# Strassen's scheme for the last matrix product of an attention and feed-forward kernel

## The chip, the cores and the metric

The kernel runs on one core of a Trainium2 chip. The metric is the device time in microseconds (us) from the start to the end of one execution. The core has a matrix engine (TensorE, PE in the rows; PEld is its weight load), a vector engine (VectorE, DVE), an activation engine (ScalarE, ACT), a general engine (GpSimd, POOL) and a queue that issues the memory transfers (SyncE, SP). Each engine works through its own instructions in a fixed order and waits at semaphores for the others.

## The reference

Attention in chunks of 64 tokens, then two feed-forward blocks on 4608 tokens of width 512:

```python
attn = softmax(q_c @ k_c.T / 8)                      # per head and chunk of 64 tokens
x = (attn @ v_c) as 4608 x 512
x = relu(x @ w_in)**2 @ w_out                        # 512 -> 2048 -> 512
x = (sigmoid(x @ w_gate) * (x @ w_val)) @ moe2_w_out # 512 -> 1536 -> 512
```

All weights come as 64-bit floats (two 32-bit words each), the result is float32. To keep float32 accuracy every operand of a product is split in two parts of a narrower float type, a high part (ScalarE, line 426) and the rest (VectorE, line 431, a subtraction with two inputs in the core's memory), and each product is three matmuls: high by high, low by high, high by low.

## The kernel before

Four products follow each other on TensorE.

- **The first** (`x @ w_in`, line 578, together with attention) runs in units of 384 tokens by Strassen's scheme in Winograd's form: seven block products, named P1 to P7, in place of eight. **The second** (line 932) is a plain product: for each of nine blocks `j` of 512 tokens, over 16 row blocks `f` of the weight, with four sums in four PSUM banks. **The third** (gate and value, line 578 again, units of 512 tokens, and one of 256) is by Strassen's scheme.
- **The last** (line 1041) is plain: for each of nine blocks `j` of 512 tokens, in falling order and block 0 at the end, for each of 12 row blocks `f` of `moe2_w_out`, a 256 KB load of `ud[f, j]` (what the third product wrote), one split, and 12 matmuls: three for each of four groups of 128 tokens. The tokens lie on the output's partitions there, so that the four sums are copied out by ScalarE and VectorE in turn (lines 411 and 1053) and stored as rows of 2 KB.

Weights pass through `to_float32` (lines 473 to 497: a 512 KB load, two operations of ScalarE, three of VectorE, one of GpSimd) and `weight_group`, which makes the Strassen sums of a pair of weight blocks on GpSimd and splits them. Those of the third product's second half and of the last product go back to memory (`through_dram`) and are loaded again when they are needed. Before, three buffers `raws2` take the loaded words in turn, and the float32 result and the sums take what the planner finds free.

What sets the order: the code states jobs (engine, cost, buffers), and `Plan` gives each a due time, counted back from TensorE's jobs, and then plays the engines through in time with estimated costs, to fix the order on each engine and the place of each buffer. A load is not placed before its `look` time ahead of its due time; `FLOOR` is memory kept free of early work. No engine reorders anything at run time.

## Time and profile before

| | us |
|---|---|
| median of 3 runs (1755.51 to 1756.17) | 1755.55 |
| the profiled execution | 1755.8 |
| its span, first to last instruction | 1754.0 |
| TensorE busy in it | 1694.7 |
| VectorE busy | 986.5 |
| ScalarE busy | 810.0 |
| GpSimd busy | 452.4 |
| the 16 transfer engines, mean | 49.7% |

The span is cut into the stretches of the four products: first 0 to 454, a passage to 545, second to 923, third to 1455, last to 1749.5. In a table of stretches each engine's busy time stands with its number of instructions, then the granted clock of TensorE (1.00 is 2.4 GHz), the transfer engines' share and what they moved.

### The profile page before, as it was taken

To read this page: it belongs to the slowest core of one execution; us is meant where nothing else is said; L and a number is where in the kernel's file an instruction comes from. 1 tells how busy PE (TensorE), PEld (TensorE's weight loads), DVE (VectorE), ACT (ScalarE), POOL (GpSimd) and SP (SyncE) were. 2 spreads that over 40 slices of the span, in tenths; PEclk is the share of its full clock that TensorE was granted. 3 is DMA by queue.
4 is the path that set the end of the run, shared out by engine and by line. 5 is a ranking of instruction groups with operands and counts; after the bars stand their busy time and mean duration, and the time that the engine had idled before them with its cause. 6 is when DMAs were issued, how large, how long until landed. Compare 5 with 4: busy or idle time off the path is not lost.

```text
span 1754.0 us, 27689 instructions
## 1 busy us (share of the span) xinstructions
PE 1694.7 (97%) x10200; PEld 1459.2 (83%) x10200; DVE 986.5 (56%) x1494; ACT 810.0 (46%) x1558; POOL 452.4 (26%) x356
## 2 busy tenths in 40 slices
PE   6789999999998999999999999999999999999998
PEld 5689999999996888888889887788788898888887
DVE  7998575766799633222277468563754553223221
ACT  6676565565685422222246445453544442222221
POOL 2653012020335300000047456452553330000000
PEclk8799999999999999999999999999999999999999
DMA  9825645554683544444455453286325553434431
GB/s 252 198 83 158 160 125 144 141 138 141 222 298 123 175 144 120 120 121 120 120 156 194 167 173 133 90 265 232 125 87 192 186 193 124 146 114 133 132 115 60
DMA packets 278488, 268.38 MB, mean 153 GB/s; under 512 B 154448, under 2 KB 204624, under 8 KB 278352
## 3 DMA queue, kind: packets, MB, share of 16 engines
q1 hardware_dynamic: 278352, 266.61, 49.7%
q8 instruction: 80, 1.31, 0.3%
q14 instruction: 56, 0.46, 0.1%
HBM read 164.30 MB, written 102.24 MB: 152 GB/s over the span
## 4 chain that ended last, share of the span: by engine, by line
PE 85%; DVE 6%; issue 2%; ACT 1%; POOL 0%; DMA 0%; DVEq 0%; ACTq 0%; POOLq 0%
PE bank L578 43%; PE bank L932 21%; PE bank L1041 17%; PE bank L722 1%; PE bank L772 1%; PE bank L756 1%; PE bank L705 0%; DVE T__823 L431 0%; DMA ud<-b__9948 0%; DVE T__11440 L431 0%; DVE T__10156 L431 0%; DVE T__10571 L431 0%; POOL yr__11118 L440 0%; DVE T__12200 L431 0%; DMA gd<-b__2780 0%
## 5 line engine op out<-in xcount | busy, mean ns | idle before, releaser
L440 POOL TENSOR_TENSOR raw__487<-raw__630,raw__487 128x384 f32<-128x384 f32 x24 | 27.6, 1170 | 251.8 <-DVE B__641 L431 195.4
L497 POOL TENSOR_TENSOR w__8576<-w__8576,raw__5243 128x512 int32<-128x512 int32 x3 | 4.4, 1454 | 271.4 <-DMA g__6439<-gd 269.7
L740 DVE TENSOR_REDUCE mx__330<-bank 128x8 f32<-128x512 f32 x16 | 11.0, 689 | 20.0 <-PE bank L722 18.3
L1041 PE MATMUL bank<-wo__6252,uop__12855 128*128 128x512 f32 x84 | 20.2, 389 | 0.0
L1041 PEld LDWEIGHTS bank<-wo__6252,uop__12855 128*128 128x128 f32 x84 | 15.8, 188 | 3.3
L497 POOL TENSOR_TENSOR w__5359<-w__5359,raw__5243 128x512 int32<-128x512 int32 x1 | 1.3, 1310 | 58.4 <-DMA gd<-e__4889 58.4
L440 POOL TENSOR_TENSOR raw__630<-raw__630 128x384 f32<-128x384 f32 x12 | 15.4, 1299 | 0.0
L1041 PE MATMUL bank<-wo__12334,uop__13151 128*128 128x512 f32 x60 | 14.4, 389 | 0.0
L1041 PE MATMUL bank<-wo__6128,uop__13397 128*128 128x512 f32 x60 | 14.4, 389 | 0.0
L440 POOL TENSOR_TENSOR raw__487<-raw__487 128x384 f32<-128x384 f32 x12 | 14.1, 1198 | 0.0
L1041 PEld LDWEIGHTS bank<-wo__12334,uop__13151 128*128 128x128 f32 x60 | 11.3, 188 | 2.3
L1041 PEld LDWEIGHTS bank<-wo__6128,uop__13397 128*128 128x128 f32 x60 | 11.3, 188 | 2.3
L787 ACT ACTIVATE raw__630<-bank 128x256 f32<-128x256 f32 x36 | 11.8, 381 | 1.5 <-PE bank L772 1.4
L787 ACT ACTIVATE raw__487<-bank 128x256 f32<-128x256 f32 x36 | 11.9, 383 | 1.0 <-PE bank L772 1.0
L1041 PE MATMUL bank<-wo__6281,uop__13350 128*128 128x512 f32 x48 | 11.5, 389 | 0.0
L1041 PE MATMUL bank<-wo__12297,uop__13135 128*128 128x512 f32 x48 | 11.5, 389 | 0.0
L1053 DVE COPY o__14742<-bank 128x512 f32<-128x512 f32 x1 | 0.7, 691 | 19.0 <-PE bank L1041 19.0
L440 DVE TENSOR_TENSOR b__9797<-b__9797,bank 128x512 f32<-128x512 f32 x6 | 4.1, 684 | 12.2 <-PE bank L578 12.2
L1041 PEld LDWEIGHTS bank<-wo__6281,uop__13350 128*128 128x128 f32 x48 | 9.0, 188 | 1.9
L1041 PEld LDWEIGHTS bank<-wo__12297,uop__13135 128*128 128x128 f32 x48 | 9.0, 188 | 1.9
L932 PE MATMUL bank<-gop__6265,wo__6128 128*128 128x512 f32 x12 | 5.4, 612 | 4.6 <-DVE gop__6265 L431 2.4
L411 ACT ACTIVATE o__13430<-bank 128x512 f32<-128x512 f32 x1 | 0.6, 598 | 19.1 <-PE bank L1041 19.1
(4427 smaller groups left out, 5605.4 us busy)
## 6 DMA issues: line engine op xcount, KB each, us to landing
g__6439<-gd SPq DMA_DIRECT2D x15, 256.0 KB, 2.7
g__6531<-gd SPq DMA_DIRECT2D x15, 256.0 KB, 2.8
g__6507<-gd SPq DMA_DIRECT2D x14, 256.0 KB, 2.9
u__12690<-ud SPq DMA_DIRECT2D x13, 256.0 KB, 3.4
u__12858<-ud SPq DMA_DIRECT2D x13, 256.0 KB, 2.7
g__6618<-gd SPq DMA_DIRECT2D x12, 256.0 KB, 2.6
ql__1102<-in_q_dram SPq DMA_DIRECT2D x80, 36.0 KB, 2.1
g__6732<-gd SPq DMA_DIRECT2D x10, 256.0 KB, 2.7
```

Of the source, the lines that this page charges most:

```text
L411: lambda: nc.scalar.activation(out=o(), in_=i(), func=func, **kw), ib, ob, soon=soon,
L440: eng, cost(eng, n), lambda: e.tensor_tensor(out=o(), in0=a(), in1=b(), op=op),
L497: nc.gpsimd.tensor_tensor(out=wi, in0=wi, in1=words()[:, :, 0], op=ALU.add)
L578: nc.tensor.matmul(out=o, lhsT=at(op, P, F32R, wi * size + half * HB + kk * P), rhs=at(xb, n, F32R, xi * xsize + off), start=(first and kk ...
L722: nc.tensor.matmul(out=o[part, 2 * hp + c, :], lhsT=qv[part, hp, tok], rhs=kv[part, hp, tok], start=True, stop=True,)
L740: job("DVE", 0.7, lambda: nc.vector.tensor_reduce(out=col8(mx, 0), in_=heads(ps), axis=AX.X, op=ALU.max), [ps], [mx])
L756: nc.tensor.transpose(out=at(ps_t, P, F32, hp * P), in_=at(a, P, F32, hp * P), identity=ident)
L772: nc.tensor.matmul(out=o[c][CH * r:CH * r + CH, hp, :], lhsT=vv[part, 2 * hp + r, :], rhs=av[part, hp, r, :], start=True, stop=True,)
L787: nc.scalar.activation(out=o[:, :, a:a + CH], in_=i, func=ACTF.Copy)
L932: nc.tensor.matmul(out=at(ps[m], BLK), lhsT=at(w1out[f], P, F32R, wi * BLK + m * P), rhs=at(op, BLK, F32R, xi * BLK), start=(f == 0 and i ...
L1041: nc.tensor.matmul(out=at(ps[m], BLK), lhsT=at(op, P, F32R, ui * BLK + m * P), rhs=at(wo[f], BLK, F32R, wi * BLK), start=(f == 0 and i == ...
L1053: job("DVE", 0.7, lambda o=o, b=ps[m]: nc.vector.tensor_copy(out=at(o), in_=at(b, BLK)), [ps[m]], [o])
```

## The change

- The last product becomes a Strassen product (`Long`). A unit is a pair of token blocks (512 tokens each) or, for block 0, two halves of 256. Its two weight halves are the row blocks 0 to 5 and 6 to 11 of `moe2_w_out` and its columns 0 to 255 and 256 to 511; each of the seven products runs over six row blocks and adds into two PSUM banks (two groups of 128 output columns), 36 matmuls. The order on TensorE is P1, P4 of the unit before, P2, P5, P6, P3, P7.
- The sums of tokens that the scheme wants are made by GpSimd (`minus`, 24 operations for a unit), and every product splits its own six operands (`x`), 42 splits for a unit.
- The output has its columns on the partitions, so VectorE turns it in blocks of 32 by 32 (line 1177), eight operations for a unit, and each turned tile is stored with four transfers whose pieces are 32 columns (128 bytes) long: 160 transfers and 73,728 pieces in all.
- `moe2_w_out` passes through `weight_group` (split sums, 6 groups of 7 x 256 KB), not `weight_rows`.
- Conversions of the third and last products' weights go through fixed buffers: two for the loaded words, two for the float32 result, one for the sums.
- Planner: the estimated transfer rate rises (190 to 270 GB/s in play, 150 to 200 for due times), `FLOOR` falls from 20 to 8 KB, loads and splits of the second product are placed later (16 and 8 us ahead, not 25), and a load of a token tile counts 25% more bytes.

```diff
-            extra = self.DMA_LATENCY + self.MARGIN + j.bytes / 150e3 if j.eng == "SP" else 0.4
+            extra = self.DMA_LATENCY + self.MARGIN + j.bytes / 200e3 if j.eng == "SP" else 0.4
...
-                dma = max(dma, t) + j.bytes / 190e3
+                dma = max(dma, t) + j.bytes / 270e3
...
-    LOOK, NEAR, HOLD, FAR, FLOOR = 60.0, 15.0, 8.0, 40.0, 20 * 1024
+    LOOK, NEAR, HOLD, FAR, FLOOR = 60.0, 15.0, 8.0, 40.0, 8 * 1024
...
-        raw = sbuf(2 * BLK, "wraw")
+        raw, w = sbuf(2 * BLK, "wraw"), sbuf(BLK, "w")
         if raws:
             turn.append(1)
-            raw = raws[len(turn) % len(raws)]
-        w = sbuf(BLK, "w")
+            raw, w = (x[len(turn) % len(x)] for x in raws[:2])
...
-        sums = sbuf(2 * BLK, "sums")
+        sums = raws[2][0] if raws else sbuf(2 * BLK, "sums")
...
+    class Long:
...
+        def product(self, ps, p, first):
...
+            if p == "P5":
+                self.minus(b11, b12, b11)
+            elif p == "P6":
+                self.minus(b11, b22, b11)
+            elif p == "P7":
+                self.minus(b12, b22, b12)
+            elif p == "P4":
+                self.minus(b21, b21, b11)
+            kind, half = A_OF[p]
+            for kp, r in enumerate(src):
+                x = Buf(8 * n, name="x", op=True)
+                split(x, r, n, look=8.0)
+                w = self.ops[kp][kind]
+
+                def go(kp=kp, x=x, w=w):
+                    size = w.size // 8
+                    for m in range(2):
+                        for i, (wi, xi) in enumerate(((0, 0), (1, 0), (0, 1))):
+                            nc.tensor.matmul(
+                                out=at(ps[m], n),
+                                lhsT=at(w, P, F32R, wi * size + half * HB + m * P),
+                                rhs=at(x, n, F32R, xi * n),
...
+            for who, p in ((u, "P1"), (last, "P4"), (u, "P2"), (u, "P5"), (u, "P6"), (u, "P3"), (u, "P7")):
...
-                dma(lambda r=r: at(r), lambda f=f, a=a: gd[f][:, a:a + BLK], src, [r], size=P * BLK * 4, look=25.0)
-                split(op, r, BLK)
+                dma(lambda r=r: at(r), lambda f=f, a=a: gd[f][:, a:a + BLK], src, [r], size=P * BLK * 4, look=16.0)
+                split(op, r, BLK, look=8.0)
...
-        raws2 = [sbuf(2 * BLK, "raw") for _ in range(3)]
+        raws2 = [sbuf(2 * BLK, "wr") for _ in range(2)], [sbuf(BLK, "wf") for _ in range(2)], [sbuf(2 * BLK, "ws")]
...
+                job("DVE", 0.1 + 0.00118 * n, lambda: nc.vector.transpose(out=at(o), in_=at(t)), [t], [o], soon=2.0)
...
+                    return [out[t0:t0 + n, m * P + 32 * g:m * P + 32 * g + 32].rearrange(
+                        "(b t) c -> t b c", t=32) for g in range(4)]
...
+                dma(dst, src, [o], size=P * n * 8, n=4, soon=2.0)
```

TensorE where the last product begins, before (`wo` is a weight block, `uop` a split token block; x3 stands for three matmuls):

```order
L578 MATMUL bank_77<-T_4096_132096__12656,vd_145408__6375 128x256 x6
L1041 MATMUL bank_73<-wo_194560__6281,uop_90112__12818 128x512 x3
L1041 MATMUL bank_78<-wo_194560__6281,uop_90112__12818 128x512 x3
L1041 MATMUL bank_75<-wo_194560__6281,uop_90112__12818 128x512 x3
L1041 MATMUL bank_76<-wo_194560__6281,uop_90112__12818 128x512 x3
L1041 MATMUL bank_73<-wo_81920__12283,uop_72704__12855 128x512 x3
```

And TensorE at the same place in the change (`x` is a split operand, `oa` a weight block's part `a`):

```order
L587 MATMUL bank_75<-T_4096_14336__12710,vd_51200__10875 128x256 x6
L895 MATMUL bank_77<-x_133120__12981,oa_198656__12302 128x512 x3
L895 MATMUL bank_76<-x_133120__12981,oa_198656__12302 128x512 x3
L895 MATMUL bank_77<-x_42496__13000,oa_86528__12315 128x512 x3
L895 MATMUL bank_76<-x_42496__13000,oa_86528__12315 128x512 x3
L895 MATMUL bank_77<-x_167936__13025,oa_116736__12324 128x512 x3
```

A split there serves six matmuls, not twelve; in the whole stretch 1296 matmuls of 512 columns become 1008 of 512 and 252 of 256.

VectorE within the last product, before (`u` is a loaded token block, `o` an output tile):

```order
L431 TENSOR_TENSOR uop_39936__13090<-u_27648__12961,uop_39936__13090 128x512
L1053 COPY o_27648__13232<-bank_78 128x512
L431 TENSOR_TENSOR uop_51200__13118<-u_37888__12724,uop_51200__13118 128x512
L1053 COPY o_55296__13252<-bank_76 128x512
L431 TENSOR_TENSOR uop_72704__12855<-u_10240__13037,uop_72704__12855 128x512
```

VectorE at the end of the first unit's P2 in the change (`e` is a sum from ScalarE's copy, to which a bank is added):

```order
L431 TENSOR_TENSOR x_90624__13140<-u_59392__12619,x_90624__13140 128x512
L440 TENSOR_TENSOR e_0__10596<-e_0__10596,bank_74 128x512
L440 TENSOR_TENSOR e_51200__13188<-e_51200__13188,bank_78 128x512
L1177 STREAM_TRANSPOSE o_122880__13267<-e_0__10596 128x512
L1177 STREAM_TRANSPOSE o_102912__13275<-e_51200__13188 128x512
L431 TENSOR_TENSOR x_42496__13000<-u_25600__12670,x_42496__13000 128x512
```

The adds wait for TensorE's P2, and the turns and the next splits stand behind them in VectorE's order.

VectorE within the second product, before (`gop` is a split block of its tokens, `y` its output):

```order
L431 TENSOR_TENSOR gop_27648__7208<-g_19456__6913,gop_27648__7208 128x512
L431 TENSOR_TENSOR gop_55296__6868<-g_15360__6439,gop_55296__6868 128x512
L944 COPY y_61440__7226<-bank_78 128x512
L944 COPY y_69632__7238<-bank_79 128x512
L431 TENSOR_TENSOR gop_23552__7029<-g_47104__6076,gop_23552__7029 128x512
```

VectorE within the second product in the change (`wr`, `wf` and `ws` are the fixed buffers of a conversion, `ga` and `vd` split weights):

```order
L489 SCALAR_TENSOR_TENSOR wf_35328__5191<-wr_29184__5130,wf_35328__5191 128x512
L431 TENSOR_TENSOR gop_37376__6455<-g_4096__6567,gop_37376__6455 128x512
L431 TENSOR_TENSOR gop_41472__6493<-g_8192__6348,gop_41472__6493 128x512
L431 TENSOR_TENSOR ga_14336__7057<-wf_6144__5270,ga_14336__7057 128x512
L431 TENSOR_TENSOR vd_8192__7062<-wf_35328__5191,vd_8192__7062 128x256
L480 TENSOR_SCALAR wf_6144__5270<-wf_6144__5270 128x512
```

Conversions moved into the second product. Of the 68, VectorE's order has 28 ahead of the first split of that product, 19 within it and 21 behind it before, and 30, 38 and none in the change.

## Rows read from the trace of the kernel before

**Rows 1.** Busy time by stretch: the four products and the passage after the first

```profile
core 0: us, PE busy (x) PEld busy (x) DVE busy (x) ACT busy (x) POOL busy (x), PEclk, DMA share, GB/s
0.00:454.00 454.00, 419.45 (x4310) 389.00 (x4311) 340.05 (x602) 283.11 (x610) 106.39 (x97) 0.96 0.60 154
454.00:545.00 91.00, 81.75 (x424) 76.95 (x423) 84.83 (x127) 70.05 (x141) 39.26 (x31) 0.95 0.77 256
545.00:923.00 378.00, 377.69 (x1655) 311.73 (x1654) 167.76 (x235) 124.79 (x210) 52.25 (x42) 0.99 0.44 133
923.00:1455.00 532.00, 521.32 (x2517) 437.79 (x2516) 313.30 (x410) 261.81 (x483) 252.75 (x186) 1.00 0.49 169
1455.00:1749.50 294.50, 294.50 (x1302) 243.71 (x1301) 79.84 (x121) 70.29 (x119) 1.73 (x2) 1.00 0.36 116
```

**Rows 2.** The chain that ended last: start, length (us), what; its end

```profile
1455.73 293.78 PE bank L1041 x1296
1749.54 0.69 DVE o__14751 L1053
```

**Rows 3.** TensorE in order of time, a unit of 256 columns: start, length, what

```profile
950.42 0.88 PE L578 MATMUL bank<-B__8743,gt__8620 128*128 128x256 f32 x6
951.14 0.88 PE L578 MATMUL bank<-T__8760,gd__6890 128*128 128x256 f32 x6
```

**Rows 4.** VectorE in order of time in the third product

```profile
1303.16 0.68 DVE L440 TENSOR_TENSOR c__9315<-c__9315,bank 128x512 f32<-128x512 f32 x1
1303.76 1.18 DVE L431 TENSOR_TENSOR T__11766<-yr__11537,T__11766 128x512 fp32r<-128x512 f32 x1
1304.86 0.68 DVE L431 TENSOR_TENSOR T__9080<-yr__11126,T__9080 128x512 fp32r<-128x512 f32 x1
1305.47 1.78 DVE L431 TENSOR_TENSOR T__10111<-yr__11560,T__10111 128x512 fp32r<-128x512 f32 x1
1307.17 1.78 DVE L431 TENSOR_TENSOR T__10546<-yr__11303,T__10546 128x512 fp32r<-128x512 f32 x1
```

**Rows 5.** GpSimd in order of time, the same stretch

```profile
1292.57 1.29 POOL L440 TENSOR_TENSOR yr__11560<-yr__11594,yr__11560 128x512 f32<-128x512 f32 x1
1293.82 1.29 POOL L440 TENSOR_TENSOR c__11620<-c__9315,c__11620 128x512 f32<-128x512 f32 x1
...
1302.65 1.74 POOL L440 TENSOR_TENSOR yr__11303<-yr__10292,yr__11303 128x512 f32<-128x512 f32 x1
...
1306.66 1.75 POOL L440 TENSOR_TENSOR yr__11126<-yr__10292,yr__11126 128x512 f32<-128x512 f32 x1
```

**Rows 6.** One stretch of the third product: line 431 alone, then line 440 alone

```profile
1240.00:1380.00 140.00, 55.41 (x53) 1.00 0.42 147
...
1240.00:1380.00 140.00, 34.19 (x51) 69.50 (x46) 1.00 0.42 147
```

**Rows 7.** VectorE's turns in attention, of 512 columns (line 688): shortest, median, longest ns

```profile
L688 DVE STREAM_TRANSPOSE qT__3114<-ql__1102 x1: 700/700/700, 260.2 to 260.2; 128x512 f32<-128x512 f32 x1
```

**Rows 8.** TensorE's longest wait in the third product, in order of time

```profile
1133.56 1.52 DVE L481 TENSOR_SCALAR w__8576<-w__8576 128x512 f32<-128x512 f32 x1
...
1138.22 0.50 PE L578 MATMUL bank<-T__10571,gs__6332 128*128 128x512 f32 x1 [2.54 <-DVE T__10571 L431]
```

**Rows 9.** Early in the second product: all engines, then line 490 (one a conversion)

```profile
545.00:590.00 45.00, 44.69 (x185) 36.01 (x184) 39.77 (x56) 21.89 (x38) 16.62 (x13) 0.94 0.48 147
...
545.00:590.00 45.00, 5.64 (x7) 0.94 0.48 147
```

**Rows 10.** SyncE issuing 16 loads in pieces of 128 bytes (attention); the last store

```profile
185.68 7.83 SPq L404 DMA_DIRECT2D ql__1770<-in_q_dram  x16
...
1750.25 0.33 SPq L404 DMA_DIRECT2D out_dram<-o__14751  x1
```

**Rows 11.** Transfers: packets, MB and share, 64 to 73 us, then 1550 to 1650 us

```profile
q1 hardware_dynamic: 6331, 1.00, 70.4%
...
q1 hardware_dynamic: 6912, 12.59, 38.7%
```

More of the change, by code (lines that the diff above doesn't have):

```diff
@@ L504, in to_float32, with weight_group @@
         return w
-    def weight_group(src, f, half, name, keep, look=None, raws=None):
-        a = to_float32(columns(src, f), f"{name}a", look, raws)
-        b = to_float32(columns(src, f + half), f"{name}b", look, raws)
-        sums = sbuf(2 * BLK, "sums")
+    def weight_group(src, f, half, name, keep, look=None, raws=None, by=None):
+        by = by or columns
+        a = to_float32(by(src, f), f"{name}a", look, raws)
+        b = to_float32(by(src, f + half), f"{name}b", look, raws)
+        sums = raws[2][0] if raws else sbuf(2 * BLK, "sums")
         ops = {}
@@ new lines, in long_units, with block_loader, get @@
+    def long_units(todo):
+        last = None
+        for make in [*todo, None]:
+            u = make() if make is not None else None
+            for who, p in ((u, "P1"), (last, "P4"), (u, "P2"), (u, "P5"), (u, "P6"), (u, "P3"), (u, "P7")):
+                if who is not None:
+                    who.stage(p)
+            last = u
+    def block_loader(load):
+        have = {}
+        def get(rc):
+            if rc not in have:
+                have[rc] = load(*rc)
+            return have[rc]
+        return get
@@ L963, in tile_attention_relu2_glu @@
                 back[m, g] = {kind: through_dram(op) for kind, op in ops.items()}
-        back_o = [through_dram(weight_rows(w2o, f, f"o{f}", keep=False, look=900.0, raws=raws2)) for f in range(F2)]
+        back_o = []
+        for f in range(G2):
+            ops = weight_group(w2o, f, G2, f"o{f}", False, look=900.0, raws=raws2, by=rows)
+            back_o.append({kind: through_dram(op) for kind, op in ops.items()})
         def tokens(s):
@@ new lines, in tile_attention_relu2_glu, with last_blocks, load @@
+        wo = [{} for _ in back_o]
+        for kind in "astd":
+            for f, b in enumerate(back_o):
+                wo[f][kind] = b[kind](look=80.0)
+        def last_blocks(s):
+            wide = len(s) == 2
+            def load(r, c):
+                out_ = []
+                for kp in range(G2):
+                    f, j, a = r * G2 + kp, s[c] if wide else 0, 0 if wide else c * HB
+                    n = BLK if wide else HB
+                    t = sbuf(n, "u")
+                    dma(lambda t=t: at(t), lambda f=f, j=j, a=a, n=n: ud[f, j][:, a:a + n],
+                        ub[f, j], [t], size=P * n * 4, look=30.0)
+                    out_.append(t)
+                return out_
+            return block_loader(load)
@@ L1059, in tile_attention_relu2_glu @@
+        long_units([
+            (lambda s=s: Long(wo, last_blocks(s), BLK if len(s) == 2 else HB,
+                              per if len(s) == 2 else per_h, finish3(s)))
+            for s in order[1]
+        ])
         plan.run()
```

112 lines of the change are left out of this document (77 added, 35 removed).

## The prediction

> **What bounds the kernel now.** I read the table of stretches first, then the chain of work that ended last, then single stretches in order of time on the engines that the change loads. In the table [rows 1] the reader is to see that TensorE has no gap in the last product: 294.50 us busy of 294.50, at the full clock of 2.4 GHz (granted 1.00), beside VectorE at 79.84, ScalarE at 70.29 and GpSimd at 1.73. The chain says the same: one piece of 1296 matmuls, 293.78 us, 0.2267 us each, and after it a copy and a store [rows 2]. So a matmul taken out there is time taken out, as long as the other engines keep up, and they have room. The second product is as full (0.31 us idle of 378). The third has 532 - 521.32 = 10.7 us of idle TensorE, the passage before the second 9.3, and the first, with attention, 34.5 [rows 1].
>
> The sums below are made against the profiled execution, 1755.8 us; the median of the three runs is 0.25 us below it.
>
> **TensorE's own work.** 1296 matmuls of 512 columns go. 1008 of 512 come, at the same form and price: 1008 x 0.2267 = 228.5 us, 57.1 for a unit of two blocks. 252 of 256 columns come for block 0; six of those begin 0.72 us after the six before them [rows 3], 0.120 each, 30.2 us in all. 293.8 - 258.7 = **35.1 us less**, for certain, if nothing makes TensorE wait.
>
> **What has to keep up.** Before, a split fed twelve matmuls, 2.7 us; now it feeds six, 1.36 us, and the sums of tokens come on top. For a unit of two blocks (57.1 us of TensorE):
>
> ScalarE: 42 splits and 8 copies, at 70.29 / 119 = 0.59 us [rows 1], 30 us. Hidden.
>
> VectorE alone: 42 splits, 6 adds and 8 turns. A split that nobody disturbs takes 0.68 and the next begins 0.61 after it; an add likewise 0.68 and 0.60 [rows 4]; a turn took 0.70 [rows 7]. 42 x 0.61 + 6 x 0.60 + 8 x 0.70 = 34.8 us. GpSimd alone: 24 subtractions of 512, one every 1.25 us [rows 5], 30 us.
>
> The two together are another matter. From 1305.47 to 1307.17 VectorE and GpSimd both had work waiting, and they took turns: a split every 1.70 us, each recorded with 1.78, and each subtraction of GpSimd with 1.75 in place of 1.29 [rows 4, 5]. So a subtraction keeps a split away for 1.70 - 0.61 = 1.09 us. The add at 1303.16 was not held up, at 0.68, beside the subtraction of 1302.65 [rows 4, 5]. The bounds for a unit are therefore: 24 x 1.70 + 18 x 0.61 = 51.8 us if all adds and turns lie beside subtractions, and 51.8 + 3.6 + 5.6 = 61.0 us if none does and both engines always have work. TensorE's 57.1 lies between them. The average case of the third product is milder: 53 splits took 55.41 us there, (55.41 - 53 x 0.68) / 46 subtractions = 0.42 us of delay for each [rows 6], which makes 34.8 + 24 x 0.42 = 44.9 us for a unit, 79% of the time; but VectorE had more free time there, and delay grows with load.
>
> The Trainium skill (SBUF — State Buffer, Who interferes with whom) states the rule: a VectorE instruction with two SBUF inputs and a GpSimd instruction that reads SBUF exclude each other for a whole instruction, while one with at most one SBUF input is not concerned. By it a unit would cost 24 x 1.25 + 42 x 0.61 = 55.6 us, the subtractions at their full undisturbed interval; the rows' 1.70 for a pair is a little under that, 1.86, so the measurement decides for 51.8. That adds go free agrees with the 0.68 above; of a turn beside GpSimd no run here shows anything.
>
> The order is sound as far as it can be read: adds stand behind the six splits of the next product, subtractions of P7 and P4 stand well ahead, and each of P1, P2 and P3 needs none. The tight place is P5 followed by P6, where the second change of b11 must wait for the splits of the first. I take **8 us of waits** for the whole last product, 3%, between 0 (all fits below 57.1) and 4 x (61.0 - 57.1) = 16, with block 0, at half sizes, taken in the same proportion; nearer the middle than nought since VectorE at 93% and 88% of a stretch went with 9.3 us of waiting in the passage [rows 1] and 0.3 early in the second product [rows 9]. What queues behind a late split: on VectorE the adds that free banks, behind these the turns, and behind those, on SyncE, the loads of the next unit's tokens.
>
> **Output transfers.** 73,728 pieces of 128 bytes are written; none is in the trace. Reads of that kind are: from 64 to 73 us 6331 packets, nearly all of 128 or 256 bytes, kept 16 engines busy for 70.4% of 9 us, 0.016 us each [rows 11]; a packet of the last product, mostly 2 KB, took 0.387 x 1600 / 6912 = 0.090 [rows 11]. At 0.016 the output costs 73,728 x 0.016 / 16 = 74 us of all engines, against 26 before (4608 packets at 0.090). The last product used 0.36 x 294.5 = 106 us of them [rows 1]; now some 155 of 267. Hidden, at price 0; a write dearer than a read is the third rival. Issue: 16 such transfers took 7.83 us, 0.49 each [rows 10]; 160 of them are 78 us of SyncE's 267, hidden too.
>
> **The end.** Before, the last store began to issue at 1750.25 and the span ended at 1754.0 [rows 10]. Now the last matmul is followed by a copy, a turn (0.4 each at 256 columns) and eight issues of 0.49, of which those of the first bank begin early: the last issue begins some 4 us after TensorE, not 0.7, but has half the bytes. **2 us more**, between 1 and 4.
>
> **Conversions.** 21 of them leave the third product. Its longest wait, 2.54 us, has a conversion as cause: at 1133.56 two of its operations held VectorE ahead of the split T__10571 [rows 8]. Other waits there come from splits and subtractions alone, which stay. Of 10.7 us I take **4 us back**, between 0 and 8. They go into the second product: 38 in 378 us, 4.5 in 45 us. Early there 7 in 45 us left TensorE 0.31 us idle, with VectorE 39.77 busy [rows 9], so the cover holds; the shorter look ahead of its loads could cost some microseconds, price 0, bounds 0 and 6. The order of the first product and the passage changes in places as the planner's estimates do: price 0, bounds -5 and +5.
>
> **The sum:** 1755.8 - 35.1 + 8 + 2 - 4 = 1726.7, say **1727 us**.
>
> **Rivals.**
>
> First, VectorE and GpSimd set the pace of the last product. For: the bound of 61.0 us, and a load on both that no stretch of the trace has for long. Against: TensorE's seven products leave time to work ahead. Then 4 x 61.0 and some 33 for block 0 make 277, that is 18 of waits: 1737, and 1745 if half of the conversions' relief and the passage go wrong too. Its mechanism is the taking of turns after 1305.47, kept up through a whole unit; it decides once more than about half of the adds and turns find no subtraction beside them.
>
> Second, more comes back than is planned: no waits in the last product, 9 us in the third and 5 in the passage. 1755.8 - 35.1 + 2 - 14 = 1709. For: the cause of [rows 8] is gone. Against: most idle time in the third product has other causes.
>
> Third, the other side: the writes of 128 bytes hold everything up. Besides output the engines have 106 - 26 = 80 us of loads, and some 14 for the larger weights. The point is where 94 + 73,728 p / 16 reaches 300 us: p = 0.045 us, about three times the small read, half of a 2 KB packet. At p = 0.048 the last product takes 315 us and the kernel 1755.8 - 293.8 + 315 + 2 - 4 = 1775, slower. Stores would pile up at SyncE and loads of tokens behind them. For: a write may cost more than a read, and only 32 partitions take part in each. Against: the factor of three. The Trainium skill (DMA: Bandwidth & Descriptors, Specifications) says that below 512 bytes a transfer becomes a read, a change and a write; if that doubled 0.016, the estimate would be 94 + 147 = 241 us, still below 267; no run here shows it.
>
> Fourth, it doesn't do what it says: matmuls are gone (the order has 1260), but the shifted order of the first and second products gives it back in new waits, 26 us of them: 1726.7 + 26 = 1753, no change.
>
> **How the numbers follow.** Chances: forecast 0.60, first rival 0.23, second 0.08, third 0.05, fourth 0.04. The range leaves out the third, the fourth and a little at each edge: **1710 to 1746**. A measurement here can tell about 0.2%, 3.5 us, from no change. Faster 0.91, same 0.03 and slower 0.06 (the third, and a bad end of the fourth).
>
> **What would show it.** In the changed kernel: line 895 at 0.227 us a matmul of 512 columns; a last product of 260 to 275 us from its first matmul to its last; VectorE at 75 to 95% and GpSimd at 50 to 65% in it; TensorE's waits there on VectorE's line 431. Waits of the third product at 3 to 8 us and no line 480 in it; the second still without gaps. Transfers at 50 to 70% in the last product. It is wrong if the transfers are at 90% or more there, if TensorE waits for loads, or if the second product opens gaps.

## The result, and the profile after

The changed kernel takes **1702.92 us** (median of four runs, 1702.39 to 1703.41), the kernel before 1755.86 beside it: a ratio of 0.9695, 95% interval 0.9679 to 0.9712. The forecast was 1727, its range 1710 to 1746. The sign was right, and the gain, 52.9 us, nearly twice the 28.8 that were forecast.

In what follows a product's time runs from its first matmul to the first of the next. The table of stretches of the changed kernel, cut there (columns as in [rows 1]):

```profile
0.00:454.00 454.00, 418.40 (x4305) 387.23 (x4306) 340.26 (x610) 284.28 (x614) 111.26 (x103) 0.97 0.60 155
454.00:518.70 64.70, 62.66 (x353) 60.57 (x352) 62.55 (x101) 57.08 (x118) 22.91 (x17) 1.00 0.82 274
518.70:910.50 391.80, 391.80 (x1731) 324.40 (x1730) 252.55 (x360) 177.37 (x315) 125.79 (x110) 1.00 0.68 220
910.50:1434.80 524.30, 520.96 (x2522) 438.80 (x2521) 252.35 (x322) 227.68 (x415) 219.36 (x153) 1.00 0.39 134
1434.80:1693.60 258.80, 258.64 (x1260) 219.10 (x1259) 236.91 (x273) 129.04 (x240) 174.08 (x118) 1.00 0.49 126
```

And the kernel before, its second and third product cut in the same way, which [rows 1] do not show:

```profile
522.40:923.00 400.60, 395.66 (x1731) 325.98 (x1730) 190.08 (x262) 143.08 (x244) 65.28 (x52) 0.99 0.45 135
923.00:1455.60 532.60, 521.92 (x2522) 438.39 (x2521) 313.83 (x412) 262.41 (x484) 253.35 (x187) 1.00 0.49 169
```

Where the 53.4 us of the two profiled spans (1754.0 and 1700.6) went:

| part | before | after | difference | forecast |
|---|---|---|---|---|
| start of the second product | 522.4 | 518.7 | -3.7 | 0 (-5 to 5), both together |
| second product | 400.6 | 391.7 | -8.9 | (0 to 6 for its looks) |
| third product | 532.6 | 524.2 | -8.4 | -4 (-8 to 0) |
| last product, to its last matmul | 293.9 | 259.3 | -34.6 | -35.1 + 8 of waits |
| from there to the end | 4.5 | 6.6 | +2.1 | +2 (1 to 4) |

The chain that ended last, where [rows 2] had one piece of 1296 matmuls:

```profile
1434.80 254.09 PE bank L895 x1221
1689.40 4.23 PE bank L895 x33
```

TensorE waits 0.16 us in the whole last product, although VectorE is busy for 92% of it (236.91 of 258.80 us). The four units of two blocks, one row each (VectorE is the third pair of numbers, GpSimd the fifth):

```profile
1434.80:1493.50 58.70, 58.70 (x261) 48.58 (x260) 58.60 (x54) 30.68 (x52) 50.74 (x32) 1.00 0.56 155
1493.50:1550.50 57.00, 57.00 (x254) 47.18 (x253) 55.04 (x57) 27.85 (x49) 40.80 (x26) 1.00 0.57 148
1550.50:1607.50 57.00, 57.00 (x253) 47.22 (x252) 53.19 (x57) 30.68 (x53) 37.62 (x24) 1.00 0.55 148
1607.50:1664.00 56.50, 56.50 (x268) 47.51 (x267) 53.02 (x70) 28.91 (x59) 36.27 (x29) 1.00 0.41 94
```

In the units VectorE is busy for 100, 97, 93 and 94%. The taking of turns is there as priced in [rows 4, 5]. First VectorE in order of time, then GpSimd:

```profile
1454.46 0.70 DVE L1177 STREAM_TRANSPOSE o__13267<-e__10596 128x512 f32<-128x512 f32 x1
...
1456.26 1.78 DVE L431 TENSOR_TENSOR x__13166<-u__12678,x__13166 128x512 fp32r<-128x512 f32 x1
1457.96 1.78 DVE L431 TENSOR_TENSOR x__13050<-u__12683,x__13050 128x512 fp32r<-128x512 f32 x1
...
1471.56 0.68 DVE L431 TENSOR_TENSOR x__13166<-u__13033,x__13166 128x512 fp32r<-128x512 f32 x1
1472.16 0.68 DVE L431 TENSOR_TENSOR x__13050<-u__12799,x__13050 128x512 fp32r<-128x512 f32 x1
```
```profile
1454.46 1.30 POOL L440 TENSOR_TENSOR u__12708<-u__13033,u__12708 128x512 f32<-128x512 f32 x1
...
1457.45 1.74 POOL L440 TENSOR_TENSOR u__12868<-u__13011,u__12868 128x512 f32<-128x512 f32 x1
```

While both have work, a split comes every 1.70 us; when GpSimd's queue is empty, from 1471.56 on, every 0.60. The turn of 1454.46 began together with a subtraction and took its 0.70 all the same. So did the others: of the product's 32 turns of 512 columns 25 lie beside a subtraction, and none of the 32 took more than 0.71. This is what the Trainium skill (SBUF — State Buffer, Who interferes with whom) says of an instruction with one SBUF input outside the two-port modes. The prediction gives the rule without that last condition, and experiment 4 shows instructions with one input that are held.

### The profile page after: what moved, and what is told of

Its sections match the earlier page's. It is cut to its first block, busy times and chain, and to the rows that moved or that the text cites. A ratio compares the mean times of both kernels' runs of the same rounds, so it can differ in the third digit from the quotient of the medians.

```text
span 1700.6 us, 28549 instructions
## 1 busy us (share of the span) xinstructions
PE 1652.8 (97%) x10164; PEld 1430.3 (84%) x10164; DVE 1145.4 (67%) x1666; ACT 876.2 (52%) x1700; POOL 653.4 (38%) x500
## 5 line engine op out<-in xcount | busy, mean ns | idle before, releaser
L496 POOL TENSOR_TENSOR wf__5191<-wf__5191,wr__5130 128x512 int32<-128x512 int32 x18 | 26.4, 1468 | 110.8 <-DVE wf__5191 L489 87.0
L496 POOL TENSOR_TENSOR wf__5270<-wf__5270,wr__5203 128x512 int32<-128x512 int32 x18 | 27.4, 1520 | 76.7 <-DVE wf__5270 L489 58.4
L440 DVE TENSOR_TENSOR b__9749<-b__9749,bank 128x512 f32<-128x512 f32 x14 | 9.6, 683 | 37.5 <-PE bank L587 37.5
L440 POOL TENSOR_TENSOR ws__5363<-wf__5270,wf__5191 128x256 f32<-128x256 f32 x18 | 17.1, 952 | 30.7 <-DVE vt__7336 L431 8.8
L749 DVE TENSOR_REDUCE mx__340<-bank 128x8 f32<-128x512 f32 x22 | 15.1, 686 | 18.9 <-PE bank L731 18.1
L440 POOL TENSOR_TENSOR ws__5363<-wf__5191 128x256 f32<-128x256 f32 x12 | 11.5, 961 | 32.9 <-DVE vs__7697 L431 15.0
L440 DVE TENSOR_TENSOR b__9566<-b__9566,bank 128x512 f32<-128x512 f32 x8 | 5.5, 684 | 20.2 <-PE bank L587 20.2
L440 POOL TENSOR_TENSOR ws__5363<-ws__5363,wf__5270 128x256 f32<-128x256 f32 x18 | 16.3, 908 | 1.4
L440 DVE TENSOR_TENSOR b__10027<-b__10027,bank 128x512 f32<-128x512 f32 x5 | 3.4, 685 | 16.4 <-PE bank L587 16.4
L473 ACT ACTIVATE wf__5191<-wr__5130 128x512 f32<-128x512 f32 x18 | 11.9, 661 | 3.4 <-POOL ws__5363 L440 2.0
L473 ACT ACTIVATE wf__5270<-wr__5203 128x512 f32<-128x512 f32 x18 | 12.0, 664 | 2.7 <-DVE va__7566 L431 0.8
L489 DVE SCALAR_TENSOR_TENSOR wf__5270<-wr__5203,wf__5270 128x512 int32<-128x512 int32 x18 | 12.9, 719 | 0.3
L496 POOL TENSOR_TENSOR w__634<-w__634,wraw__342 128x512 int32<-128x512 int32 x1 | 1.3, 1297 | 29.6 <-DMA wraw__374<-in_moe_w_in_dram 29.6
L489 DVE SCALAR_TENSOR_TENSOR wf__5191<-wr__5130,wf__5191 128x512 int32<-128x512 int32 x18 | 12.4, 688 | 0.2
L477 ACT ACTIVATE wr__5203<-wr__5203 128x512 int32<-128x512 uint32 x18 | 12.1, 669 | 0.0
L411 ACT ACTIVATE b__9749<-bank 128x512 f32<-128x512 f32 x14 | 8.4, 597 | 7.1 <-PE bank L587 6.5
L477 ACT ACTIVATE wr__5130<-wr__5130 128x512 int32<-128x512 uint32 x18 | 12.0, 666 | 0.0
```

What stands on the lines that cost most here:

```text
L411: lambda: nc.scalar.activation(out=o(), in_=i(), func=func, **kw), ib, ob, soon=soon,
L440: eng, cost(eng, n), lambda: e.tensor_tensor(out=o(), in0=a(), in1=b(), op=op),
L473: nc.scalar.activation(out=at(w), in_=t[:, :, 1].bitcast(F32), func=ACTF.Abs)
L477: nc.scalar.activation(out=low, in_=low.bitcast(U32), func=ACTF.Copy, scale=2.0**-29)
L489: nc.vector.scalar_tensor_tensor(out=wi, in0=words()[:, :, 1], scalar=-0x40000000, in1=wi, op0=ALU.bitwise_and, op1=ALU.bitwise_or,)
L496: nc.gpsimd.tensor_tensor(out=wi, in0=wi, in1=words()[:, :, 0], op=ALU.add)
```

## Experiments

In each, "last" and so on are the products' times in the profiled execution, "total" the median of the runs, and the ratio is taken against the kernel before, run beside it, whose medians lie between 1756.4 and 1759.5. A name in brackets is the version's, by which later sections call it.

**1. Is it Strassen's scheme alone?** The changed kernel with the plain last product of before (plain_last):

```diff
...
-            ops = weight_group(w2o, f, G2, f"o{f}", False, look=900.0, raws=raws2, by=rows)
-            back_o.append({kind: through_dram(op) for kind, op in ops.items()})
+        back_o = [through_dram(weight_rows(w2o, f, f"o{f}", keep=False, look=900.0, raws=raws2)) for f in range(F2)]
...
```

> The changed kernel with the last product plain as before (and its weights converted as plain rows); fixed buffers and the planner's new numbers stay, and so does the place of the conversions: 30 before the second product, 38 within it, none behind it. Theory (two separate gains: 35.0 us of matmuls in the last product, less 2.5 at the end; and 20.9 us ahead of it, from where the conversions stand): the last product takes 293.8 us again and begins at 1435 as in the changed kernel, so 1702.9 + 35.0 - 2.5 = 1735 us; third product 524 us, second 392. Rival (the early gain hangs on the Strassen last product, through the memory that it leaves free or takes): the last product begins at 1450 or later, 1750 us or more.

Measured: second 391.7, third 525.3, last 293.9, total 1734.93 (ratio 0.9861, 0.9832 to 0.9889). So 21 of the 53 us (1755.9 - 1734.9; 24 against the kernel before beside it) have nothing to do with the last product: buffers and planner give them. The scheme itself gives 32, net of its longer end.

**2. Which of the planner's numbers?** First the looks of the second product back to 25 us and none (no_look):

```diff
-                dma(lambda r=r: at(r), lambda f=f, a=a: gd[f][:, a:a + BLK], src, [r], size=P * BLK * 4, look=16.0)
-                split(op, r, BLK, look=8.0)
+                dma(lambda r=r: at(r), lambda f=f, a=a: gd[f][:, a:a + BLK], src, [r], size=P * BLK * 4, look=25.0)
+                split(op, r, BLK)
```

> The changed kernel with the second product's loads and splits placed as early as before (25 us ahead, splits without a limit). In its order 20 conversions stand behind the second product again. Theory (conversions in the third product cost it 8 us): the third product takes 530 to 534 us, not 524; the last stays at 259 us, for it has no wait to lose; the time is 1709 to 1713 if the second product keeps its 392 us, up to 1720 if it waits again at its start. Rival (the conversions' place is of no account, the shorter look is what helped): third product 524 still, second 400: 1711 too, told apart by the stretches.

Measured: start 519.1, second 391.7, third 529.9, last 259.3, total 1708.28 (0.9709, 0.9681 to 0.9737). The looks are worth 5 us, all in the third product; that conversions are the reason, as the theory has it, keep_20 below does not bear out. Then the transfer rates, the token loads' size and `FLOOR` back (no_rate):

```diff
-            extra = self.DMA_LATENCY + self.MARGIN + j.bytes / 200e3 if j.eng == "SP" else 0.4
+            extra = self.DMA_LATENCY + self.MARGIN + j.bytes / 150e3 if j.eng == "SP" else 0.4
...
-                dma = max(dma, t) + j.bytes / 270e3
+                dma = max(dma, t) + j.bytes / 190e3
...
-    LOOK, NEAR, HOLD, FAR, FLOOR = 60.0, 15.0, 8.0, 40.0, 8 * 1024
+    LOOK, NEAR, HOLD, FAR, FLOOR = 60.0, 15.0, 8.0, 40.0, 20 * 1024
...
-        dma(o, i, writes=[r], size=P * H * D * 5, n=1, look=look)
+        dma(o, i, writes=[r], size=P * H * D * 4, n=1, look=look)
```

> The changed kernel with the planner's old estimates (150 and 190 GB/s, 20 KB kept free, token tiles at their size). In its order 20 conversions stand behind the second product again. Theory: third product 530 to 534 us, last 259, time 1709 to 1720. Rival: the estimates themselves made the early gain, then the first product and its passage are as before (second product begins at 522, takes 400) and the third takes 524.

Measured: start 525.6, second 400.4, third 534.2, last 270.3, total 1736.81 (0.9871, 0.9837 to 0.9906). Start and second product are as the rival had them, the rest neither had: all of the extra gain goes, and the last product takes 11 us more besides, with 6.7 us of waits, near the forecast's 8. Next `FLOOR` alone back to 20 KB, which leaves 20 conversions behind the second product as before (keep_20):

> The changed kernel with 20 KB kept free of early work, as before, the rates and look-aheads new. In its order 28 conversions stand before the second product, 20 within it, 20 behind it. Theory (rates clear the start of the second product, memory kept free decides on the conversions): second product from 518 us, 392 long; third 529 to 535; last 259 to 262; whole 1708 to 1714. Rival (the memory kept free does both): second product 398 or more, whole 1717 to 1723.

Measured: second 391.7, third 525.5, last 259.3, total 1702.83 (0.968, 0.9657 to 0.9704): no difference to the changed kernel in the total, and 1.3 us in the third product, where the theory had 5 or more. That the conversions leave the third product is worth next to nothing. Now single parts put into the kernel before; the fixed buffers alone (fix_only):

> The kernel before with nothing but the fixed buffers of the conversions. In its order 26 conversions stand before the second product, 20 within it and 22 behind it, so they hardly move. Theory (the place counts, not the buffers): the third product takes 530 to 535 us, the time is 1745 to 1760. Rival (fixed buffers by themselves give the gain, as the change's description has it): 1735 us.

Measured: second 397.8, third 534.6, last 294.0, total 1755.25 (0.9975, 0.9962 to 0.9989): 0.25%, at the edge of what can be told. The new rates and load size alone (rate_only):

```diff
-            extra = self.DMA_LATENCY + self.MARGIN + j.bytes / 150e3 if j.eng == "SP" else 0.4
+            extra = self.DMA_LATENCY + self.MARGIN + j.bytes / 200e3 if j.eng == "SP" else 0.4
...
-                dma = max(dma, t) + j.bytes / 190e3
+                dma = max(dma, t) + j.bytes / 270e3
...
-        dma(o, i, writes=[r], size=P * H * D * 4, n=1, look=look)
+        dma(o, i, writes=[r], size=P * H * D * 5, n=1, look=look)
```

> The kernel before with nothing but the planner's new transfer rates and token sizes (the memory kept free stays at 20 KB); in its order 26 conversions stand before the second product, 22 within it, 20 behind it. Theory (these estimates are what takes the waits out of the start of the second product): it begins at about 518 us and takes 392, with third product 530 to 534 and last 294: 1755.9 - 12.5 = 1743 us. Rival (it takes memory kept free or the shorter look to do it): second product 398 to 401 us, whole 1750 to 1758.

Measured: start 517.7, second 391.7, third 535.8, last 294.0, total 1745.94 (0.9934, 0.9889 to 0.9979). The rates alone bring the whole 12 us of the passage and the second product, and none of the third, which takes 3 us longer. Last, the scheme and the fixed buffers with the planner's old numbers and looks (strassen_fix):

> The Strassen last product and the fixed buffers, with all of the planner's numbers and look-aheads as before. In its order 26 conversions stand before the second product, 20 within it, 22 behind it. Theory (the last product's gain is its own 35 us, the early 21 us are the planner's numbers'): second product from 522 to 526 us and 398 to 401 long, third 530 to 536, last 259 to 271 (with the old rates it waited 11 us in the run with the old estimates): 1720 to 1735 us, near what was forecast. Rival (Strassen and fixed buffers bring the early gain too): 1705 us or less.

Measured: second 397.9, third 530.1, last 271.4, total 1729.54 (0.9832, 0.9808 to 0.9856): near the forecast, because there the last product does take 12 us more than its matmuls need, and the second and third give back 2.7 and 2.5 us. Of these 12 us 7.5 are waits, all but 0.2 of them in the first unit; the rest is matmuls that follow each other more slowly after them, in part at the lower clock (0.50 for two stretches of 3.4 us). The whole product, TensorE's longest wait, and VectorE and GpSimd in order of time around it:

```profile
1450.10:1721.60 271.50, 263.91 (x1262) 221.16 (x1260) 233.75 (x272) 130.00 (x241) 174.76 (x122) 0.99 0.48 126
```
```profile
1480.71 1.71 PE L895 MATMUL bank<-x__13135,os__12711 128*128 128x512 f32 x4 [3.39 <-DVE x__13135 L431]
```
```profile
1477.23 1.75 DVE L431 TENSOR_TENSOR x__13054<-u__12964,x__13054 128x512 fp32r<-128x512 f32 x1
1478.91 1.75 DVE L431 TENSOR_TENSOR x__13135<-u__12666,x__13135 128x512 fp32r<-128x512 f32 x1
```
```profile
1451.26 1.73 POOL L440 TENSOR_TENSOR u__12654<-u__12818,u__12654 128x512 f32<-128x512 f32 x1
...
1480.07 1.72 POOL L440 TENSOR_TENSOR u__12766<-u__12766,u__12673 128x512 f32<-128x512 f32 x1
```

GpSimd begins the first unit's subtractions at 1451.26, after that product's first matmul (1450.1), and then works without a pause past 1481; a split comes every 1.69 us while TensorE uses one in 1.36, and the stock runs out. In the changed kernel the first of them stands 8 us ahead of the product (first matmul 1434.6), and five are begun by then:

```profile
1426.60 1.74 POOL L440 TENSOR_TENSOR u__12619<-u__12799,u__12619 128x512 f32<-128x512 f32 x1
```

In no_rate, too, they begin after the product's first matmul (1461.6 and 1460.2). That the early start is what spares the changed kernel the waits is read from these rows; no run moves the subtractions alone.

**3. How much room is left?** Each output tile turned twice (turn_twice), then three times (turn_thrice):

```diff
-                job("DVE", 0.1 + 0.00118 * n, lambda: nc.vector.transpose(out=at(o), in_=at(t)), [t], [o], soon=2.0)
+                job("DVE", 0.1 + 0.00118 * n, lambda: [nc.vector.transpose(out=at(o), in_=at(t)) for _ in range(2)], [t], [o], soon=2.0)
```

> The changed kernel, each of the 40 turns of the output done twice; the order of everything else is the same. Measured in the changed kernel: VectorE is busy 236.9 of the last product's 258.8 us, and TensorE waits 0.16 us there. A turn costs 0.65 us (19.44 us for 30). Theory (VectorE really is that full, and the cover is 22 us of idle time that lies mostly in the last units): 24 us are added, most of them still hidden; the last product takes 260 to 272 us, the whole 1704 to 1715. Rival (its busy time is largely waiting for GpSimd, which shrinks when VectorE asks less often, so there is much more cover than it seems): last product 259 to 260 us, 1703.

> The changed kernel, each turn done three times, the order otherwise the same. Theory: 48 us more for VectorE, 285 of 259, so at least 26 us show, and more where TensorE's clock falls after waits: last product 283 to 300 us, whole 1727 to 1745. Rival: waiting for GpSimd absorbs it: last product 259 to 268, whole below 1713.

Measured: last 268.0 and 282.3, totals 1712.37 (0.9727, 0.9684 to 0.9771) and 1726.84 (0.9809, 0.9763 to 0.9856). A turn more for every tile, 5.2 us of VectorE in a unit (8 x 0.65) and some 25 us in all, costs 8.7 us, the next 14.3. (Of the 8.7 and 23.0 us in all, the traces show 3.6 and 13.6 as waits of TensorE.) So VectorE had room for about 17 of the first 25 us and 11 of the next. The three turns end 1 us below what the theory had and 14 above the rival, which has a share in it: VectorE's busy time grows by 25 us for 51 us of turns (262.2 for 237.1), since line 431 falls from 199 to 173 us. Three turns with GpSimd's subtractions 8 columns wide (turn_thrice_small) tell whether the subtractions are what fills it:

```diff
-                binary("POOL", self.words(oo), self.words(xx), self.words(yy), ALU.subtract,
-                       self.n, [oo], {oo, xx, yy})
+                job("POOL", cost("POOL", self.n), lambda oo=oo, xx=xx, yy=yy: nc.gpsimd.tensor_tensor(
+                    out=at(oo, 8), in0=at(xx, 8), in1=at(yy, 8), op=ALU.subtract),
+                    [*{oo, xx, yy}], [oo], shared=True)
```

> As the run with three turns, and GpSimd's subtractions of tokens in the last product cut to 8 columns of 512 or 256 (so their time goes, and their place, waits and partners stay; it computes something else). Theory (splits and subtractions keep each other waiting): line 431 falls from 187 us for 180 splits to 0.68 each, 122 us; VectorE has 236.9 - 60 + 48 = 225 us, below 259: last product 259 to 262 us, whole 1703 to 1707. Rival (splits are long for another reason, transfers or TensorE's reads): line 431 stays above 170 us and the whole is as slow as with three turns alone.

Measured: last 259.3, total 1702.53 (0.9671, 0.9627 to 0.9716): the 23 us are gone. TensorE's greatest wait with three turns; then line 431 alone in the four units, in the changed kernel and in this one:

```profile
PE bank L895 <- DVE x__13405 L431: 5.6, 3, 1.9
```
```profile
1434.80:1664.00 229.20, 187.24 (x180) 1.00 0.52 136
```
```profile
1434.80:1664.00 229.20, 105.01 (x172) 1.00 0.53 138
```

A split takes 1.04 us beside full subtractions and 0.61 beside short ones. Subtractions keep VectorE from its splits for a third of these units: (187.2 - 180 x 0.61) / 229 = 34%.

**4. What did the third product wait for?** Three kernels with the order and the places of before, on every engine, and some instructions cut to 8 columns: the conversions' operations on VectorE and GpSimd (conv_small); the third product's subtractions of tokens (third_small); both (both_small).

```diff
+        c = 8 if raws else BLK
...
-            nc.vector.tensor_scalar_max(at(w), at(w), TINY)
+            nc.vector.tensor_scalar_max(at(w, c), at(w, c), TINY)
...
```

> The kernel before, with the same order on every engine; only VectorE's three operations and GpSimd's one of each conversion that goes through the three buffers of loaded words (second, third and last products' weights) are cut from 512 columns to 8, so that the weights' values are not the reference's. Theory: these instructions, standing ahead of splits that TensorE needs, cause the waits. The third product falls from 532.6 to 523 to 527 us, the second from 400.6 to 391 to 395, the start of the second from 522 to 517 to 520; total 1736 to 1744 us. Rival: the order of the other work causes them (loads, splits, sums of weights, buffers that come free late); the stretches stay within 2 us of before and the total at 1750 to 1757.

```diff
-                binary("POOL", part(oo), part(xx), part(yy), ALU.subtract, n, [oo[0]], {oo[0], xx[0], yy[0]})
+                c = 8 if oo[0].name.startswith("yr") else n
...
+                    out=at(oo[0], c, F32, oo[1]), in0=at(xx[0], c, F32, xx[1]), in1=at(yy[0], c, F32, yy[1]), op=ALU.subtract),
...
```

> The kernel before, with the same order and places on every engine; only GpSimd's subtractions of token blocks in the third product are cut from 512 columns to 8, so that the output is not the reference's. Theory: VectorE's splits wait for those subtractions, and TensorE for the splits, so the third product falls from 532.6 to 522 to 526 us, as in the changed kernel (524.2), and the total to 1745 to 1750 us. Rival: something else makes these waits (copies out of the banks, sums of weights, the conversions together with them); the third product stays at 530 to 533 and the total at 1753 to 1757.

> third_small and conv_small together: the subtractions of the third product and the conversions' operations on VectorE and GpSimd cut to 8 columns, order and places unchanged; the output is not the reference's. Theory: if each alone leaves a part, the two together bring the third product to 520 to 525 us and the second to 397; total 1738 to 1746 us. Rival: the third product stays at 530 or more even then, so that the waits come from the order of the copies out of the banks and of TensorE's own work; total 1748 to 1754.

Measured: third 532.2, 524.6 and 524.5 us; second 397.1, 400.6 and 397.1; totals 1753.63 (0.9981, 0.997 to 0.9992), 1747.73 (0.9924, 0.9885 to 0.9963) and 1746.73 (0.9928, 0.9888 to 0.9968). The profile of conv_small is of its fastest run, 4.7 us below the median. The wait of [rows 8] with short conversions (2.54 us before), and the third product with short conversions, then with short subtractions:

```profile
PE bank L580 <- DVE T__10571 L431: 1.0, 1, 1.0
```
```profile
916.50:1448.90 532.40, 522.49 (x2522) 438.48 (x2521) 282.77 (x412) 262.72 (x484) 226.72 (x185) 1.00 0.49 168
```
```profile
922.90:1447.50 524.60, 520.35 (x2522) 438.87 (x2521) 279.61 (x412) 262.11 (x484) 175.37 (x185) 1.00 0.49 170
```

With short conversions that wait shrinks by 1.5 us, one of 0.7 opens right behind it, and the product ends no sooner. With short subtractions 8.0 us go, as many as the changed kernel saves (8.4), and TensorE's waits there fall from 10.7 to 4.3 us. What remains are waits below 1.1 us, most of them on copies out of the banks.

The wait of [rows 8] shows how the two hang together. VectorE in order of time, ahead of the split that TensorE waits for: before, with short conversions, with short subtractions:

```profile
1133.56 1.52 DVE L481 TENSOR_SCALAR w__8576<-w__8576 128x512 f32<-128x512 f32 x1
1135.11 1.39 DVE L483 TENSOR_SCALAR w__8576<-w__8576 128x512 int32<-128x512 int32 x1
```
```profile
1127.10 1.26 DVE L484 TENSOR_SCALAR w__8576<-w__8576 128x8 f32<-128x8 f32 x1
1128.39 1.21 DVE L485 TENSOR_SCALAR w__8576<-w__8576 128x8 int32<-128x8 int32 x1
```
```profile
1130.13 0.41 DVE L481 TENSOR_SCALAR w__8576<-w__8576 128x512 f32<-128x512 f32 x1
1130.58 0.43 DVE L483 TENSOR_SCALAR w__8576<-w__8576 128x512 int32<-128x512 int32 x1
```

The conversion's two operations read one tensor each, and subtractions held them as they hold splits: 1.52 and 1.39 us beside them, 0.41 and 0.43 without. Cut to 8 columns they still took 1.26 and 1.21, so at this place conv_small did not make them short; third_small left them whole, and the wait was gone. So most of the third product's waits were VectorE's work held by GpSimd's subtractions, and the changed order, which has them all, no longer lets them reach TensorE. Which rows of its order do it was not followed; it takes the new rates and the shorter looks together, since no_look stands at 529.9 and no_rate at 534.2, and neither rates nor fixed buffers alone do it (535.8 and 534.6). The fixed buffers were not taken out alone.

In the second product the conversions do count: it takes 3.5 us less with short ones (397.1 in both kernels that have them, 400.6 without).

The subtractions cut in the same way in the last product of strassen_fix (strassen_fix_small):

> The kernel strassen_fix (Strassen in the last product, fixed buffers, the old estimates, looks and FLOOR), same order; GpSimd's subtractions of token blocks in the last product cut from 512 columns to 8, so that the last product's output is not the reference's. Theory: the taking of turns of VectorE and GpSimd makes the 12 us of waits of its last product; that stretch falls from 271.4 to 259 to 261 us and the total from 1729.5 to 1717 to 1720. Rival: loads or the order of VectorE's other work cause them; the last product stays at 268 to 272 and the total at 1726 to 1730.

Measured: last 262.7 in place of 271.4, total 1722.74 (0.9792, 0.9754 to 0.983). Of the 12 us more 8.7 are the subtractions'; it lies between the two expectations. Of the other 3.4 us 1.9 are waits, 1.5 of these on ScalarE's half of a split (line 426); what delays that half was not followed.

**5. The end.** The changed kernel once more (after_again), and beside it a version that issues the last eight stores on SyncE's and ScalarE's queues by turns (two_queues):

```diff
...
+                        for g, (a, b) in enumerate(zip(dst(), src())):
+                            (nc.scalar if g % 2 else nc.sync).dma_start(out=a, in_=b)
...
```

> The changed kernel itself, beside the next: 1702 to 1704 us, 7.0 us from its last matmul to the end of the span.

> The changed kernel, of the last eight stores every second one issued by ScalarE, which is idle by then. Theory (issue at 0.46 us each is what the end waits for: the last one is issued 4.6 us after the last matmul): four issues go beside four, so 1.8 us less after the last matmul, 5.2 for 7.0, whole 1701. Rival (a store's own landing sets the end, or the two queues take turns): within 0.5 us of the changed kernel.

Measured: 1703.42 (0.9683, 0.9666 to 0.97) and 1700.91 (0.967, 0.9651 to 0.9689). From the last matmul to the end it is 5.0 us, not 6.6. The issues in the changed kernel, then in this one:

```profile
1694.59 1.79 SPq L404 DMA_DIRECT2D out_dram<-o__15418  x4
1696.48 1.87 SPq L404 DMA_DIRECT2D out_dram<-o__15420  x4
```
```profile
1695.13 1.15 SPq L1190 DMA_DIRECT2D out_dram<-o__15420  x2
1695.16 0.96 ACTq L1190 DMA_DIRECT2D out_dram<-o__15420  x2
```

Counted from the last matmul's end, the last issue ends 1.7 us earlier (2.7 us for 4.4), and so does the span. By its median it is the fastest of all versions. The 1.7 us are what the trace shows. The rest of the 2.5 is not shown to be the edit's: in the two profiles it lies ahead of the second product, where nothing was changed, and the intervals against before overlap.

## Why the prediction was wrong, step by step

- **TensorE's own work, right.** 293.9 - 259.3 = 34.6 us measured for 35.1.
- **Waits in the last product, mis-sized: 8 forecast, 0.2 measured.** The load was judged well: VectorE 53 to 58.6 us in a unit, between the bounds of 51.8 and 61.0, and 92% over the product. (GpSimd came to 67%, a little above the 50 to 65.) What failed is the step from load to waiting: the 8 us were taken between the bounds of the load, and the head start of the splits was not priced. VectorE made nobody wait at 92%, for its results came ahead of their use, and the order decided that: with the old rates the same instructions made the product 11 to 12 us longer, with 6.7 and 7.5 us of waits (no_rate, strassen_fix). That the subtractions begin before the product is the likely reason in that order. The forecast's own price was near that of an order it did not have.
- **Conversions, the cause that failed.** The forecast took its 4 us for the third product from the one longest wait [rows 8] and said that the other causes, splits and subtractions, "stay". It was the reverse: to take the conversions out or make them short was worth 0.4 to 1.3 us there (conv_small, keep_20), to make the subtractions short 8 us (third_small), and the new order hid them. The two operations ahead of T__10571 were long themselves because subtractions held them, 1.52 and 1.39 us for 0.41 and 0.43; the forecast took an instruction with one SBUF input to be free of that.
- **Passage and second product, the step that took the time out of the range: priced at 0 within 5, measured 12.5.** The forecast called the second product as full as the last, from the row 545 to 923 [rows 1]. Its first matmul is at 522.4, and its waits lie at 541 to 544, which that cut counts to the passage; the granted clock of 0.94 in [rows 9] is their trace. TensorE before, in order of time, a short stretch with the granted clock (the number after GpSimd's), and VectorE ahead of the second wait:

```profile
541.16 0.73 PE L932 MATMUL bank<-gop__6265,wo__6128 128*128 128x512 f32 x2 [2.22 <-ACT gop__6265 L426]
544.31 4.63 PE L932 MATMUL bank<-gop__6265,wo__6128 128*128 128x512 f32 x10 [2.41 <-DVE gop__6265 L431]
```
```profile
544.30:548.80 4.50, 4.49 (x11) 3.53 (x12) 4.47 (x6) 2.95 (x5) 2.09 (x2) 0.50 0.01 2
```
```profile
540.74 1.51 DVE L481 TENSOR_SCALAR w__6368<-w__6368 128x512 f32<-128x512 f32 x1
542.29 0.83 DVE L483 TENSOR_SCALAR w__6368<-w__6368 128x512 int32<-128x512 int32 x1
543.04 1.21 DVE L431 TENSOR_TENSOR gop__6265<-g__6010,gop__6265 128x512 fp32r<-128x512 f32 x1
```

  The two halves of one late split cost 4.6 us of waiting, and after it the clock stood at 0.50, its lower level (1.2 GHz), so that ten matmuls took 4.63 us, not 2.27. VectorE's half stood behind a conversion, and with short conversions that wait is 0.4 us; ScalarE's half is as late as before there (2.2). 1728 x 0.2267 = 391.7 us is what the second product needs; it took 400.6. The sum was there to be made. The other 3.7 us lie ahead of it: a wait of 2.77 us at 462.29, which with the new rates gives way to two of 0.5. rate_only shows that the order alone takes all of this away; which of its rows do it was not followed. Without this step the sum would have held: 1726.7 - 7.8 - 4.4 = 1714.5, inside the range.
- **The end, right** (+2.1 for +2). **Transfers, hidden as forecast, and cheaper:** the writes cost 0.012 us a piece, not 0.016 (below), and the transfer engines stood at 49%, not at 155 of 267 us, 58%.
- **The rivals.** The second, with 1709, had nearly the right terms (no waits, 9 in the third product, 5 in the passage) and a chance of 0.08. It was called unlikely because most idle time in the third product "has other causes": true, but those were not fixed either. The range went wrong with the passage's bound of 5, which the rival kept too.

## What to carry to other kernels

Where a planner's estimates change with the work, all of TensorE's waits in the old trace are up for change, not only those whose instructions the diff names: price every stretch's distance from matmuls times their interval as something that a new order can give back or lose. A wait's last cause is no proof of its worth: make the suspected instructions short in the unchanged order, look in the new trace whether they did become short, and see whether the stretch ends sooner. And a neighbour engine that is busy for 92% of a stretch is a risk to price by how far ahead of use its results come, not a cost by itself.

## What was not expected of the hardware

**Writes of 128 bytes** cost no more than reads of that size. All transfers of the changed kernel from 1460 to 1660 us (packets, MB, share of 16 engines):

```profile
q1 hardware_dynamic: 69975, 27.54, 53.0%
DMA packets 69990, 27.72 MB, mean 139 GB/s; under 512 B 58455, under 2 KB 61527, under 8 KB 69975
```

The trace has each packet's size and time. Of the 58,455 below 512 bytes 55,287 are pieces of 128 bytes, at 0.0119 us each in the mean; the others have 4 bytes and take 0.009. In the kernel before, from 64 to 73 us [rows 11], 4287 reads of 128 bytes took 0.0129 each and 1772 of 256 bytes 0.0244: the forecast's 0.016 was the mean over both sizes. By the byte a piece of 128 costs 1.9 times a packet of 2 KB (8448 of them in the same 200 us, at 0.0999). The Trainium skill (DMA: Bandwidth & Descriptors, Specifications) has a read, a change and a write below 512 bytes; no surcharge of the writes over reads of the same size is seen here.

**A short wait can cost twice, and need not.** After 2.22 and 2.41 us of waiting TensorE ran at half its clock for 4.5 us, as shown above. After 2.54 us at 1138.22 [rows 8] it did not (granted 1.00 from there to 1142.7). The wait of 2.77 us at 462.29 stands in six of the profiles, at the same instruction and with 2.76 to 2.78 us: in three the granted clock right after it was 0.50, in three 1.00. The kernel before, then fix_only, 4.5 us from that wait's end:

```profile
462.30:466.80 4.50, 4.50 (x14) 4.50 (x15) 2.88 (x6) 2.30 (x6) 1.30 (x1) 0.50 0.82 258
```
```profile
465.40:469.90 4.50, 4.48 (x26) 4.49 (x27) 4.28 (x8) 3.82 (x8) 1.38 (x2) 1.00 0.79 264
```

So the same wait is followed by 14 matmuls in one execution and by 26 in another, and a few microseconds between two executions can come from that alone.
